# All attention scores from float32 words, with a head's two halves of keys on the two halves of the array's rows

## The chip, the cores and the metric

The kernel runs on one core of a Trainium2 chip. A core has TensorE (PE, matrix products out of on-chip memory SBUF into the accumulators PSUM), VectorE (DVE), ScalarE (ACT), GpSimd (POOL), a queue that issues transfers (SP), and 16 DMA engines that carry them. Each engine works through its own list of instructions in order and waits at semaphores for the others. The metric is the device time of one execution, in microseconds (us). The kernel before took 1036.89 us (median of 3 runs, 1036.31 to 1038.67).

## The reference

Attention of 4 batches x 8 heads, 576 queries and keys, 64 numbers to a head, with a threshold on the scores; then two layers, each a product into 2048 columns, a function, and a product back to 512 columns. All in float32.

```python
scores = scale * np.matmul(q, k.transpose(0, 1, 3, 2))           # 4 x 8 x 576 x 576, 64 terms to a sum
thresh = np.max(scores, axis=-1, keepdims=True) - tau
scores = np.where(scores >= thresh, scores, -1000000000.0)
attn = np.exp(scores - np.max(scores, axis=-1, keepdims=True))
attn = attn / (np.sum(attn, axis=-1, keepdims=True) + 1e-09)
x = np.matmul(attn, v)                                            # heads side by side: 2304 x 512
h = x @ w_in;   sp = log1p(exp(h));   x = (h * tanh(sp)) @ w_out  # first layer
h = x @ w_in2;  x = (h * clip(h + 3, 0, 6) / 6) @ w_out2          # second layer
```

A score that is slightly wrong can fall on the other side of the threshold, so the scores are computed to float32's precision. The other products use pairs of float16 numbers (a high and a low part, three products).

## The kernel before

**A planner sets the order.** Every piece of work is a task with the engines that may do it, a cost, the tasks it needs, the buffers it holds and a due time (lines 150 to 330). `Plan.run` takes the tasks in the order of a model of the engines and writes each engine's list accordingly. The constants at the top of the file (`STEP`, `START`, `EASE`, `WHO` and so on) are due times and weights of this planner; `BUFS`, `PV_DEEP` and `BANKS` are the numbers of buffers. A buffer's next user waits until its last reader is done. The trace has the lists as they then ran.

**Attention** goes batch by batch, in each through four pairs of heads. A pair has four blocks of 128 queries, two tiles each (one per head), and a block with the last 64 queries of both heads, one tile: 9 tiles a pair, 36 a batch, 144 in all. A tile passes: scores on PE (`scores`, L1479) into a buffer `s` of two banks, 288 keys in each; maximum on DVE (`peak`, L1488); threshold and exponential on ACT (L1493, L1498); mask and sum on DVE (`mask`, L1501), which frees `s`; a float16 high part on ACT (L1506) and a low part on POOL (`p_lo`, by the helper at L387); a transposing DMA (L1514) that turns the tile's keys into rows (`pt`); and the product with the values on PE (`pv`, L1527, 28 products for two heads). There are two buffers `s`, three each of `e` and `p16`, two of `pt`. Normalised blocks are flipped (L1643) into the input of the first layer.

**The scores were computed in two ways.** In batch 0 (`direct`), q and k are loaded as float32 on rows 0 to 63 of the array and multiplied as they are: one float32 product for each half of the keys. In batches 1 to 3, q and k are loaded twice, one copy on each half of the rows, and split into a high and a low part in a shorter format (`float32r`): `k_hi` and `q_hi` on ACT (L1391, L1384), `q_lo` on DVE or POOL (the helper L387), `k_lo` on DVE (L1394). With the parts stacked on 128 rows, two products for each half of the keys give the same precision: four a tile.

**The first layer** runs behind the attention. Products with `w_in` (`gemm1`, L865) are dealt out in small pieces between the attention's products, block by block of 256 tokens as they come out; their results go to DRAM (`hd`). Once the attention is over come the function (Mish) and the products with `w_out` (`gemm2`, L979), then the second layer (L1052, L1199). Weights arrive as 64-bit words and are converted on DVE, ACT and POOL (`convert`, `one_conversion`, L446 to L600). Those of `w_out` (`convert(1, ...)`) lie in memory that the attention's buffers of the pool `early` had held, so that their conversion can begin only when batches 0 to 2 are planned.

## Time and profile before

| | us |
|---|---|
| median of 3 runs | 1036.89 (1036.31 to 1038.67) |
| the profiled execution | 1039.59 |
| its span, first to last instruction | 1037.4 |
| PE busy | 959.5 (92%) |
| DVE busy | 776.5 (75%) |
| ACT busy | 672.2 (65%) |
| POOL busy | 548.5 (53%) |
| attention, start of its last scores in the trace | 428.8 |

Busy time counts an instruction from its start to its end. PE's products overlap in the pipeline, so how many it can do is read from the distance between their starts, not from the length of one. TensorE's clock is either at 2.4 GHz or at 1.2 GHz; the profile's column PEclk is the granted share of the higher one.

### The profile page before, as it was taken

Reading aid. Unit: us, or ns where it says so; the run is one execution under the profiler, and the core shown is the slowest. Engines: PE = TensorE matmul, PEld = TensorE weight load, DVE = VectorE, ACT = ScalarE, POOL = GpSimd, SP = SyncE. Lnnn points to the kernel's source line nnn. Section 1 sums busy time; section 2 is a strip of 40 time slices with the busy share of each in tenths; the row PEclk is TensorE's granted clock in tenths of the full one; section 3 lists DMA queues with packets and bytes.
Section 4 is the critical chain, followed back from the end, with each engine's and each line's share of the span. In section 5 each row is a group of like instructions: output and inputs, shape, how many; then the busy total and the mean of one; then the engine's idle time right before and its main releaser. Section 6 shows DMA issues by size and latency. Waiting matters only on the chain.

```text
span 1037.4 us, 25967 instructions
## 1 busy us (share of the span) xinstructions
PE 959.5 (92%) x10776; PEld 853.8 (82%) x10776; DVE 776.5 (75%) x1454; ACT 672.2 (65%) x1058; POOL 548.5 (53%) x421
## 2 busy tenths in 40 slices
PE   4879898999898998899999999989899999999996
PEld 2556577888788877798888888889899999999986
DVE  5887787887877879768888889889647747746754
ACT  5666587788788878666778787736436435536542
POOL 1667666566666567663667788742323324224332
PEclk9996689999999999899999999999999999999998
DMA  9685769999999999987656565753011101101001
GB/s 269 187 173 133 180 147 245 200 236 221 221 226 222 207 243 226 211 297 255 227 199 219 207 251 199 259 215 143 21 38 57 38 22 58 57 2 57 22 2 42
DMA packets 199333, 166.83 MB, mean 161 GB/s; under 512 B 174128, under 2 KB 174640, under 8 KB 192816
## 3 DMA queue, kind: packets, MB, share of 16 engines
q1 hardware_dynamic: 199216, 165.18, 60.2%
q8 instruction: 85, 1.39, 0.6%
q14 instruction: 32, 0.26, 0.1%
HBM read 86.64 MB, written 36.04 MB: 118 GB/s over the span
## 4 chain that ended last, share of the span: by engine, by line
PE 65%; DMA 12%; DVE 10%; ACT 4%; issue 4%; POOL 3%; SPq 0%; DVEq 0%; POOLq 0%; ACTq 0%
PE y_y L979 16%; DMA pt_tr<-p_ph 10%; PE h_g L865 10%; PE s_s L1479 7%; PE h_g0a L1052 4%; PE hp_g1a L1052 4%; PE aux_pv L1527 3%; POOL p_ph L387 2%; PE hp_g1d L1052 2%; PE h_g0d L1052 2%; DVE e_ex L1501 1%; PE h_g1b L1052 1%; ACT e_ex L1498 1%; PE y_y__1_8_0_15376 L1199 1%; PE y_y___1_1_0_11177 L1199 1%
## 5 line engine op out<-in xcount | busy, mean ns | idle before, releaser
L387 POOL TENSOR_TENSOR p_ph<-e_ex,p_ph 128x128 f16<-128x128 f32 (+3 forms) x160 | 187.1, 1191 | 103.2 <-ACT p_ph L1506 84.6
L387 POOL TENSOR_TENSOR gs_h<-g_ab,gs_h 128x896 f16<-128x896 f32 x36 | 94.5, 2639 | 219.4 <-ACT gs_h L1149 219.1
L1052 PEld LDWEIGHTS <-w__h 128*128 128x128 f16 x2016 | 157.5, 98 | 7.6 <-issue 6.9
L1199 PEld LDWEIGHTS <-gs_h 128*128 128x128 f16 x1512 | 146.4, 98 | 18.0 <-DVE out_va L1243 1.4
L1488 DVE TENSOR_REDUCE nm_pk<-s_s 128x1 f32<-128x576 f32 x144 | 105.2, 750 | 37.7 <-PE s_s L1479 37.0
L1501 DVE SCALAR_TENSOR_TENSOR e_ex<-s_s,thr_th,e_ex 128x576 f32<-128x576 f32 x144 | 111.9, 812 | 21.5 <-ACT thr_th L1493 16.5
L1498 ACT ACTIVATE e_ex<-s_s,nm_pk 128x576 f32<-128x576 f32 x144 | 104.3, 733 | 24.4 <-DVE nm_pk L1488 15.2
L1527 PE MATMUL aux_pv<-vh,pt_tr 128*128 128x65 f16 (+1 forms) x1296 | 89.9, 206 | 23.2 <-DMA pt_tr<-p_ph 21.8
L1527 PEld LDWEIGHTS <-pt_tr 128*128 128x128 f16 x2016 | 83.4, 104 | 33.7 <-DMA pt_tr<-p_ph 29.2
L1506 ACT ACTIVATE p_ph<-e_ex 128x576 f16<-128x576 f32 x144 | 94.9, 680 | 15.1 <-DVE e_ex L1501 7.0
L1052 PEld LDWEIGHTS <-w__u 128*128 128x128 f16 x1008 | 99.2, 98 | 1.0 <-issue 1.0
L1149 ACT ACTIVATE gs_h<-g_ab 128x1792 f16<-128x1792 f32 x36 | 59.9, 1690 | 38.0 <-DVE g_ab L387 38.0
L1133 ACT ACTIVATE g_ab<-g_ab,aux,hscales 128x512 f32<-128x512 f32 x72 | 54.1, 804 | 20.6 <-DVE g_ab L1080 20.6
L913 ACT ACTIVATE he_t<-h_g,hin 128x512 f32<-128x512 f32 x69 | 47.2, 685 | 23.3 <-PE h_g L865 19.4
L387 DVE TENSOR_TENSOR gs_h<-g_ab,gs_h 128x896 f16<-128x896 f32 x36 | 48.5, 1350 | 17.7 <-ACT gs_h L1149 17.7
L1080 DVE TENSOR_TENSOR g_ab<-h_g0d,s_ka 128x256 f32<-128x256 f32 x36 | 13.6, 419 | 58.9 <-PE h_g0d L1052 41.2
L959 DVE SCALAR_TENSOR_TENSOR gs_h<-hp_e,fscales,gs_h 128x512 f16<-128x512 f32 x72 | 51.4, 742 | 6.6 <-ACT gs_h L953 6.6
L1139 DVE SCALAR_TENSOR_TENSOR g_ab<-g_ab,f 128x512 f32<-128x512 f32 x72 | 52.5, 767 | 2.5 <-ACT g_ab L1133 2.5
L1479 PE MATMUL s_s<-kda_lk,qsa_qp 64*128 64x288 f32 x80 | 36.5, 618 | 19.0 <-DVE e_ex L1501 9.4
L950 ACT ACTIVATE hp_e<-hl_l 128x512 f32<-128x512 f32 x72 | 41.5, 593 | 15.8 <-DVE gs_h L959 15.6
L953 ACT ACTIVATE gs_h<-hp_e,fscales 128x512 f16<-128x512 f32 x72 | 46.2, 679 | 7.2 <-PE y_y L979 5.1
L446 DVE TENSOR_REDUCE top<-raw_lr 128x1 f32<-128x1024 f32 x32 | 38.9, 1215 | 10.1 <-DMA raw_lr<-in_moe_w_out 5.5
(691 smaller groups left out, 2927.2 us busy)
## 6 DMA issues: line engine op xcount, KB each, us to landing
hd<-he_t SPq DMA_DIRECT2D x36, 512.0 KB, 3.7
hl_l<-hd SPq DMA_DIRECT2D x18, 1024.0 KB, 5.3
raw_lr<-in_moe_w_in SPq DMA_DIRECT2D x16, 1024.0 KB, 5.5
raw_lr<-in_moe_w_out SPq DMA_DIRECT2D x16, 1024.0 KB, 6.7
yd<-yl_zhy SPq DMA_DIRECT2D x9, 896.0 KB, 3.8
rk_lk<-in_k SPq DMA_DIRECT2D x12, 576.0 KB, 5.4
rq_lq<-in_q SPq DMA_DIRECT2D x12, 576.0 KB, 5.9
v_lv<-in_v SPq DMA_DIRECT2D x16, 320.0 KB, 5.8
```

Of the source, the lines that this page charges most:

```text
L387: engine[e].tensor_tensor(dst, a, b, ALU.subtract)
L865: mm(hv[:, j, :], wj[:, wl, c * P : (c + 1) * P], x.tile[:, c, xl, :], start=j == 0 and n == 0, stop=j == 1 and n == 11, skip_group_check= ...
L979: mm(yv[:, h, :], wt[1][f // 2].tile[:, f % 2, wl, c * P : (c + 1) * P], gs[fp // COL].tile[:, fp % COL, gl, f % 2, :], start=fp == 0 and ...
L1052: mm(dst.tile[:, i * Q : (i + 1) * Q], wt[2][fp][wl].tile[:, right - 1, c * P : (c + 1) * P], x[xl].tile[:, c, left - 1], start=first and ...
L1149: nc.scalar.activation(part.tile[:, :, 0], g.tile[:, :, 1:], AF.Copy)
L1199: mm(region(p), part[:, gl, left - 1], wt[3][fp][wl].tile[:, right - 1], start=fp == n == 0 and spot(p)[1] == 0, stop=fp == NG - 1 and n == 2,
L1479: mm(s[j].tile[:, half, :HALF], lh, rh[:, half * HALF : (half + 1) * HALF], start=m == 0, stop=m == len(terms) - 1,)
L1488: nc.vector.tensor_reduce(neg.tile[:, j : j + 1], sv(j), AX.XY, ALU.max, negate=True)
L1498: nc.scalar.activation(ev(j), sv(j), AF.Exp, bias=neg.tile[:, j : j + 1])
L1501: nc.vector.scalar_tensor_tensor(ev(j), sv(j), thr.tile[:, j : j + 1], ev(j), ALU.is_ge, ALU.mult)
L1506: nc.scalar.activation(p16.tile[:, js, :S], e_.tile[:, js], AF.Copy)
L1527: mm(ov[:, dst, :d], pt.tile[:, j, ch, :], part.tile[:, src, vc, :], start=i == j == ch == 0 and part is vh, stop=j == w - 1 and ch == 8, ...
```

## The change

All 144 score tiles are now products of float32 words. k is laid out so that the first 288 keys of a head stand on rows 0 to 63 and the last 288 on rows 64 to 127; q stands on both halves. The two halves of the keys are then two products on the two halves of the array's rows, each into its own bank. The splitting into parts goes, with its buffers; k's load is half as large (288 KB a pair), q's stays at 576 KB, in batch 0 too (288 KB before). k is still multiplied by the scale on ACT, in half as many columns. The memory that this frees holds the converted `w_out` from the start, so that its conversion is no longer tied to the end of batch 2. The buffers `e` and `p16` go from 3 to 4, `pt` from 2 to 3. Batch 3 is planned like the others. The planner's constants have new values.

```diff
-PV_DEEP = 2
+PV_DEEP = 3
-BUFS = {"e": 3, "p16": 3}
+BUFS = {"e": 4, "p16": 4}
...
-    early = ExitStack()
-    ep = early.enter_context(tc.tile_pool(name="early", bufs=1, side="right"))
+    wpool_o = ctx.enter_context(tc.tile_pool(name="wpool_o", bufs=1))
...
-    r_rq = ring("rq", ap, 1, [P, 2, S])
-    r_rk = ring("rk", ap, 1, [P, 2, S])
-    r_qs = [ring("qs" + "ab"[k], (ap, ep)[k], 2, [P, 2, QW], F32R) for k in range(2)]
-    r_kd = [ring("kd" + "ab"[k], (ap, ep)[k], 2, [P, 2, S], F32R) for k in range(2)]
-    r_kld = [ring("kld" + "ab"[k], (ap, ep)[k], 2, [P, 2, S], F32R) for k in range(2)]
+    r_qs = ring("qs", ap, NPAIR, [P, 2, QW])
+    r_kd = ring("kd", ap, NPAIR, [P, 2, HALF])
...
+        def load_k(e):
+            nc.sync.dma_start(out=kd.tile, in_=k[n])
+        def load_q(e, js):
+            nc.sync.dma_start(out=qs.tile[:, js, :S], in_=q[n][:, js])
         def k_scaled(e):
-            nc.scalar.activation(words(kd), words(kd), AF.Copy, scale=qscale[:D])
+            nc.scalar.activation(kd.tile, kd.tile, AF.Copy, scale=qscale)
...
-            kh = prep({"act": 1.2}, k_hi, [lk], [rk, kd], "kh")
-            a = prep({"act": 1.155}, lambda e: q_hi(slice(0, 2)), [lq], [rq, qs], "qh")
-            for j in range(2):
-                ql.append(prep(both(S), lambda e, j=j: q_lo(e, j), [a], [rq, qs], f"ql{j}_"))
-            kl = prep({"dve": 1.42}, k_lo, [kh], [rk, kd, kld], "kl")
+        kl = prep({"act": 0.65}, k_scaled, [lk], [kd], "kh")
...
             def scores(j):
-                if direct:
-                    qt, ks = qs.tile[:D].bitcast(F32), [kd.tile[:D].bitcast(F32)]
-                else:
-                    qt, ks = qs.tile, [kd.tile, kld.tile]
                 if c < NQ:
                     q0 = j * TAIL + c * P
-                    terms = [(qt[:, j, q0 : q0 + P], k[:, j]) for k in ks]
+                    terms = [(qs.tile[:, j, q0 : q0 + P], kd.tile[:, j])]
...
-                for half in range(2):
-                    for m, (lh, rh) in enumerate(terms):
+                for m, (lh, rh) in enumerate(terms):
+                    for half, r in enumerate(side):
                         mm(
                             s[j].tile[:, half, :HALF],
-                            lh,
-                            rh[:, half * HALF : (half + 1) * HALF],
+                            lh[r],
+                            rh[r],
...
-    plan.run(before)
-    early.close()
-    wpool_o = ctx.enter_context(
-        tc.tile_pool(name="wpool_o", bufs=1, side="right", reuse_waits="tile")
-    )
-    convert(1, w1o, wpool_o, plan.clock["dve"] + OUT_AT, OUT_STEP * STEP, r_h)
+    convert(1, w1o, wpool_o, START + OUT_AT * STEP, OUT_STEP * STEP, r_h)
```

`side` is the pair of row ranges 0 to 63 and 64 to 127.

In PE's list, a place in batch 1 of the kernel before: a block's last products with the values, the scores of the block's two heads (`s_s_..._0_...` and `s_s_..._1_...`), and first-layer products.

```order
L1527 MATMUL aux_pv_4_0_1_1784<-vh_140,pt_tr_4_0_1_1668 128x130
L1479 MATMUL s_s_1_0_0_1803<-kda_kh_1_1255,qsa_qp_0_1095 128x288
L1479 MATMUL s_s_1_0_0_1803<-klda_kl_2_1508,qsa_qp_0_1095 128x288
L1479 MATMUL s_s_1_0_0_1803<-kda_kh_1_1255,qsa_qp_0_1095 128x288
L1479 MATMUL s_s_1_0_0_1803<-klda_kl_2_1508,qsa_qp_0_1095 128x288
L1479 MATMUL s_s_1_1_0_1814<-kda_kh_1_1255,qsa_qp_0_1095 128x288
L1479 MATMUL s_s_1_1_0_1814<-klda_kl_2_1508,qsa_qp_0_1095 128x288
L1479 MATMUL s_s_1_1_0_1814<-kda_kh_1_1255,qsa_qp_0_1095 128x288
L1479 MATMUL s_s_1_1_0_1814<-klda_kl_2_1508,qsa_qp_0_1095 128x288
L865 LDWEIGHTS w__h_6__1_1357
L865 MATMUL h_g_0_0_0_1_1687<-x_fl_0_2_438,w__h_6__1_1357 128x256
```

The same kind of place in the changed kernel's list, for the two heads of a block (`s_s_3_0_...` and `s_s_3_1_...`).

```order
L1486 MATMUL aux_pv_2_0_1_2805<-vh_136,pt_tr_2_1_1_2696 128x65
L1438 MATMUL s_s_3_0_0_2836<-kd_lk_0_1235,qs_qp_0_1230 128x288 x2
L860 LDWEIGHTS w__h_2__1_698
L860 MATMUL h_g_0_0_2_1_2801<-x_fl_0_2_1984,w__h_2__1_698 128x256
L860 LDWEIGHTS w__h_2__1_698
L860 MATMUL h_g_0_0_2_1_2801<-x_fl_0_2_1984,w__h_2__1_698 128x256
L1438 MATMUL s_s_3_1_0_2848<-kd_lk_0_1235,qs_qp_0_1230 128x288 x2
L860 LDWEIGHTS w__h_2__1_698
```

A tile's scores are two calls in place of four, and the two heads stand apart, with first-layer products between them. Counted over the whole list, the scores stood in 84 unbroken groups before, 20 of them in batch 0 and 64 in batches 1 to 3; now in 112, of 21, 29, 31 and 31 in the four batches, and 78 of them hold one tile. The calls number 80 a batch now; before 80 in batch 0 and 160 in each of the others.

In DVE's list, the first work of the kernel before: the maxima of the values (`vt_vm`) and of the first scores (`nm_pk`).

```order
L373 COPY istack<-ident 64x64
L1333 TENSOR_REDUCE vt_vm_0_1_194<-v_lv_0_0_168 128x1
L1488 TENSOR_REDUCE nm_pk_0_0_1_200<-s_s_0_0_0_182 128x1
L1333 TENSOR_REDUCE vt_vm_0_1_194<-v_lv_0_0_170 128x1
L1333 TENSOR_REDUCE vt_vm_0_1_194<-v_lv_0_0_172 128x1
L1333 TENSOR_REDUCE vt_vm_0_1_194<-v_lv_0_0_174 128x1
L1488 TENSOR_REDUCE nm_pk_0_0_1_200<-s_s_0_1_0_191 128x1
```

And that of the changed kernel.

```order
L371 COPY istack<-ident 64x64
L1447 TENSOR_REDUCE nm_pk_0_0_1_197<-s_s_0_0_0_186 128x1
L1447 TENSOR_REDUCE nm_pk_0_0_1_197<-s_s_0_1_0_192 128x1
L1460 SCALAR_TENSOR_TENSOR e_ex_0_0_2_205<-s_s_0_0_0_186,thr_th_0_0_1_208,e_ex_0_0_2_205 128x576
L1324 TENSOR_REDUCE vt_vm_0_1_212<-v_lv_0_0_177 128x1
```

The first scores' maxima and the first mask now stand ahead of the values' maxima.

In SP's list, transfers of the changed kernel at the end of batch 0 and in batch 1: the last load of `w_in` and the first of `w_out` (`raw_lr`), loads of k, q and v, transposes.

```order
L509 DMA raw_lr_7_0_1244<-in_moe_w_in 128x1024
L509 DMA raw_lr_0_0_1251<-in_moe_w_out 128x1024
L1342 DMA v_lv_2_0_1299<-in_v 128x640
L1631 DMA td<-xts_fl_4_2_1310 128x64
L1473 DMA_TRANSPOSE pt_tr_3_1_1_1351<-p_ph_3_0_1_1222 128x18x128
```

The first load of `w_out` now stands in the list as early as the end of batch 0, the next three up to the end of batch 1, the other four in batch 3; before, all eight stood in batch 3, the last two behind the attention's last transpose. On DVE the conversion of `w_out` has 16 long steps (two a group, the lines that were L567 and L572): 13 of them now stand ahead of the attention's last mask, 8 of these between the 50th and the 84th of its 144 masks; before, 6 of the 16, from the 125th mask on.

## Rows read from the trace of the kernel before

**Rows 1.** Stages: busy PE, PEld, DVE, ACT, POOL; clock, DMA share, GB/s.

```profile
0.00:145.00 145.00, 110.44 (x695) 77.09 (x696) 109.01 (x213) 92.04 (x150) 84.28 (x89) 0.85 0.72 181
145.00:437.00 292.00, 266.66 (x3266) 238.37 (x3267) 230.09 (x404) 237.01 (x430) 190.63 (x169) 0.98 1.06 222
437.00:690.00 253.00, 250.16 (x2365) 224.58 (x2363) 214.20 (x387) 182.86 (x269) 176.35 (x127) 1.00 0.67 235
690.00:750.00 60.00, 54.15 (x767) 51.35 (x764) 47.79 (x101) 31.25 (x43) 16.37 (x8) 0.97 0.26 94
750.00:1038.00 288.00, 278.10 (x3694) 262.44 (x3691) 175.40 (x353) 129.02 (x167) 80.87 (x30) 0.99 0.12 37
```

**Rows 2.** Who waited for whom, 145 to 437 us: total us, times, longest.

```profile
PEld L1527 <- DMA pt_tr<-p_ph: 25.9, 21, 2.7
PE aux_pv L1527 <- DMA pt_tr<-p_ph: 19.0, 19, 2.4
```

**Rows 3.** DMA, 145 to 437 us: packets, MB, share; issues, KB, landing us.

```profile
q1 hardware_dynamic: 137075, 64.22, 105.0%
...
raw_lr<-in_moe_w_out SPq DMA_DIRECT2D x5, 1024.0 KB, 7.1
...
pt_tr<-p_ph SPq DMA_TRANSPOSE x62, 5.5
```

**Rows 4.** Scores by form: count, shortest/median/longest ns, first and last start.

```profile
L1479 PE MATMUL s_s<-kda_lk,qsa_qp x80: 402/684/847, 6.9 to 104.3; 64*128 64x288 f32 x80
L1479 PE MATMUL s_s<-kdb_lk,qsb_qp x80: 402/684/846, 38.4 to 144.5; 64*128 64x288 f32 x80
L1479 PE MATMUL s_s<-kda_kh,qsa_qp x140: 288/297/589, 158.6 to 428.8; 128*128 128x288 f32 x140
```

**Rows 5.** PE by time, batch 0: start, length, line, tiles, shape, count.

```profile
102.19 0.38 PE L865 MATMUL h_g<-x_fl,w__h__1_420 128*128 128x256 f16 x2
102.50 2.20 PE L1479 MATMUL s_s<-kda_lk,qsa_qp 64*128 64x288 f32 x8
104.55 1.13 PE L1479 MATMUL s_s<-kdb_lk,qsb_qp 64*128 64x288 f32 x4
105.61 0.61 PE L865 MATMUL h_g<-x_fl,w__h__1_420 128*128 128x256 f16 x4
```

**Rows 6.** The same view, an earlier stretch of batch 0.

```profile
31.86 4.17 PE L1479 MATMUL s_s<-kda_lk,qsa_qp 64*128 64x288 f32 x8 [1.44 <-DVE e_ex L1501]
```

**Rows 7.** The same view, batch 1.

```profile
209.30 0.38 PE L1479 MATMUL s_s<-kda_kh,qsa_qp 128*128 128x288 f32 x1
209.51 0.29 PE L1479 MATMUL s_s<-klda_kl,qsa_qp 128*128 128x288 f32 x1
...
210.31 0.29 PE L1479 MATMUL s_s<-klda_kl,qsa_qp 128*128 128x288 f32 x1
210.44 0.61 PE L865 MATMUL h_g<-x_fl,w__h__1_1357 128*128 128x256 f16 x4
```

**Rows 8.** Chain that ended last, 0 to 145 us, shares by line.

```profile
by line: PE s_s L1479 30.4%; issue 8.0%; PE h_g L865 6.7%; DVE e_ex L1501 6.0%; DMA kdb_lk<-in_k 6.0%; PE aux_pv L1527 5.4%; DMA raw_lr<-in_moe_w_in 5.3%; POOL p_ph L387 3.9%; DMA pt_tr<-p_ph 3.3%; DVE nm_pk L1488 2.6%; SPq L1405 1.6%; POOL
```

**Rows 9.** Splitting of k and q, and batch 0's scaling of k, by form.

```profile
L1391 ACT ACTIVATE kda_kh<-rk_lk,qscale x8: 1240/1256/1260, 86.4 to 378.1; 128x1152 fp32r<-128x1152 f32 x8
L1384 ACT ACTIVATE qsa_qp<-rq_lq x7: 1150/1161/1181, 133.1 to 380.7; 128x1152 fp32r<-128x1152 f32 x7
L1394 DVE SCALAR_TENSOR_TENSOR klda_kl<-rk_lk,qscale,kda_kh x8: 1406/1408/1529, 112.9 to 379.4; 128x1152 fp32r<-128x1152 f32 x8
L1408 ACT ACTIVATE kda_lk<-kda_lk,qscale x2: 1254/1254/1254, 5.4 to 8.2; 64x1152 f32<-64x1152 f32 x2
```

**Rows 10.** The low part of q on POOL.

```profile
L387 POOL TENSOR_TENSOR qsa_qp<-rq_lq,qsa_qp x14: 1403/1413/2272, 140.1 to 387.5; 64x576 fp32r<-64x576 f32 x14
```

**Rows 11.** Conversion of weights on DVE, two of a group's three long steps.

```profile
L446 DVE TENSOR_REDUCE top<-raw_lr x32: 1202/1214/1226, 18.3 to 665.0; 128x1 f32<-128x1024 f32 x32
L567 DVE SCALAR_TENSOR_TENSOR cvt_c__1_329<-raw_lr,cvt_c__1_329 x1: 1215/1215/1215, 38.9 to 38.9; 128x1024 uint32<-128x1024 uint32 x1
```

154 lines of the change are left out of this document (60 added, 94 removed).

## Prediction

> **What bounds the kernel now.** I read the stages first [rows 1]. From 437 us on PE does little but work: 250.2 us busy of 253, and 278.1 of 288 after 750. What is left there is first- and second-layer products, whose number does not change. Only the attention, up to 437, and the short dip from 690 to 750 (54.2 of 60) can move. So I ask of each edit: how many microseconds sooner or later does PE get through the attention with the products dealt out in it?
>
> The two parts of the attention differ. Batch 0 takes 145 us, a later batch 292 / 3 = 97. In batch 0 the scores alone are 30.4% of the chain that ends last, 44 us [rows 8]. Their float32 records are 64 rows high, two to each product: the 160 records [rows 4] answer to 80 products. At the higher clock four of them take 1.13 us, the last with its 0.40 us to the end, so they start (1.13 - 0.40) / 3 = 0.243 us apart [rows 4, 5]; at 31.86 us eight take 4.17, or 0.52 each [rows 6], the lower level of the two (1.2 and 2.4 GHz), in a stretch where PE had just waited 1.44 us for DVE; over all of batch 0 the granted clock is put at 0.85 [rows 1]. A tile of four records is 0.97 us at the higher clock and about 2 at the lower.
>
> In batches 1 to 3 no engine is full and none is idle: PE 266.7 of 292, ACT 237.0, DVE 230.1, POOL 190.6 [rows 1]. The DMA share is 1.06, and the transposes land 5.5 us after their issue [rows 3]; PE's longest waits are for them, 19 times 19.0 us in all, seen also at its weight loads [rows 2]. So PE has about 25 us of slack there, made by transposes that come late.
>
> **Fewer float32 records in a row: batch 0.** The two halves of the keys now stand on different rows. If PE works on both halves at once, and takes its list in order, then a lone tile, whose records stand as half 0, half 0, half 1, half 1, can overlap only the second with the third: three slots of 0.243 us for four. In a longer group each neighbouring pair of unequal halves overlaps, so that m products take m + 1 slots, where they took 2m. No row shows two halves at once, so the bounds are the nearest rows: no overlap (2m slots, as now [rows 5]) and complete overlap (m). I take m + 1, since it needs only that neighbours on different rows overlap.
>
> The Trainium skill ("TensorE: Matmul & The Clock Gate", Part 3) says that matmuls on different row groups run at the same time and start in program order, some 4 ns apart; no run here shows it.
>
> In batch 0 the changed list has 80 products in 21 groups: 101 slots for 160. The chain's 44 us become 44 x 101 / 160 = 28, a gain of 16 us. No overlap gives 0, complete overlap 44 / 2 = 22. What is late next is DVE: 109.0 us of work [rows 1] in 145 - 16 = 129 us, a share of 84%, above the 79% of the later batches. The list lets DVE start on scores before it waits for the values, which helps it to that share. So I let the 16 stand; at 22 it would have to reach 89%.
>
> **More PE time in batches 1 to 3.** There a product of split parts is one record on 128 rows, 0.133 us apart; eight of them, entry included, take 210.44 - 209.30 = 1.14 us, so entry costs at most 1.14 - 8 x 0.133 = 0.08 [rows 7]. All of it: 480 x 0.133 + 64 groups x 0.08 = 69 us. The 64-row records have a dearer entry: the product before them starts at about 102.30 (the second of two, 0.11 apart), its 0.11 us end at 102.41, the next one after twelve records starts at 105.61; 3.20 - 12 x 0.243 leaves 0.28 us for entry and exit [rows 5]. The changed list has 240 products in 91 groups: (240 + 91) x 0.243 + 91 x 0.28 = 80 + 25 = 106 us. That is 37 us more for PE.
>
> The Trainium skill ("TensorEngine Tiling (Array Packing)", Key Properties) says that a change of tiling mode drains TensorE, which speaks against a list that goes to and fro 112 times. The trace agrees so far as the exit costs too: the last record starts at 104.55 + 3 x 0.243 = 105.28 and is over at 105.52, 0.09 us before the next product [rows 5]. By the rule the sum is as above; if only the first float32 weight load cost, the 0.19 us that are left, it would be 8 us less.
>
> Behind each score group wait first-layer pieces and products with the values on PE's list, and behind the latter the flips. What covers the 37 us is the slack of 25 us; I charge the rest, +12. Bounds: with complete overlap the cost is 240 x 0.243 + 25 - 69 = +15, which the slack covers: 0. With none it is 480 x 0.243 + 25 - 69 = +73, less 25: +48. If the slack covers nothing, +37. Deeper buffers (`e`, `p16`, `pt`) let more transposes be under way; since the DMA engines are at a share of 1.06 already, I give that nothing, but it is the reason why the slack may shrink without cost.
>
> **What goes from the other engines.** ACT loses 12 x (1.25 + 1.16) and 4 x 1.25 us and gets 16 scalings of half the columns, by the row of 1.25 us for 1152 about 0.63 each (an estimate): 34 - 10 = 24 us less. DVE loses 12 x 1.41 = 17, POOL 24 x 1.41 = 34 [rows 9, 10]. But half of it comes back: 7 of the 16 long steps of `w_out`'s conversion move into the attention, 3.5 groups with three steps of 1.2 us each on DVE [rows 11], 13 us, and as much again on ACT and POOL together. The loads: ten of k in the window lose 288 KB each, 2.9 MB of 64, and some three or four of `w_out` at 1 MB come in [rows 3]; so the DMA share stays. None of these engines sets the pace in batches 1 to 3 beside PE and the transposes, so 0; the bounds are -12 (the relief gives back what is charged above) and +4 (1 MB more where the share is over 1, at 222 GB/s 4.5 us).
>
> **The dip from 690 to 750.** It is where the second layer starts while DVE still converts and splits: DVE 47.8 of 60 busy, PE 5.9 idle [rows 1]. The 13 us of conversion that leave the stretch after 437 let that work end sooner: -4, bounds 0 and -6. The end, after 750, has new constants but the same work: 0, within 3 either way.
>
> **Sum.** -16 + 12 - 4 = -8. On the profiled execution, 1037.4 us of span and 2.2 around it, that is 1039.6 - 8 = 1031.6. The median of the runs lies 2.7 below that execution, and the forecast is given on the runs' scale: 1029 us.
>
> **Rivals.** Under 0.2% (2.1 us) this kernel's measurement can't tell a change from none.
>
> 1. *Overlap in order, slack used* (the forecast): 1029, by itself 1014 to 1044. Chance 0.47, of it 0.36 faster, 0.04 same, 0.07 slower.
> 2. *Complete overlap.* The halves run side by side even in a lone tile. Batch 0 gains up to 22, batches 1 to 3 lose nothing: 1036.9 - 22 - 4 = 1011. For it: the order of the four records may not matter if each half of the rows has its own queue. Against it: DVE's 109 us in batch 0. Chance 0.18, all faster.
> 3. *PE becomes the bound of batches 1 to 3* (slower). Place: the 91 score groups there. Price: the 37 us show in full, because the waits for late transposes [rows 2] fall at other times than the extra records; it decides from the point where slack hides less than 17 of them, since then more than the 20 us gained elsewhere show. -16 + 37 - 4 = +17: 1054. For it: PE is already the busiest engine, and lone tiles pay entry and exit each. Chance 0.17.
> 4. *No overlap*, the change does not do what it says: the halves run one after the other as two 64-row records each. Batch 0 gains nothing, batches 1 to 3 lose 48, the dip gives 4: +44, 1081. For it: nothing in the trace shows two records at once, and a float32 record may fill a resource that both halves need. Chance 0.13.
> 5. *The transposes set the pace throughout* [rows 2, 3], and batch 0's gain is lost in later waits: 1036. Chance 0.05, nearly all same.
>
> Together: faster 0.36 + 0.18 = 0.54; same 0.04 + 0.04 = 0.08; slower 0.07 + 0.17 + 0.13 + 0.01 = 0.38. The range takes in cases 1, 2 (at its likely end) and 3 with 12 us beyond it, and leaves out case 4 and the tails: 1008 to 1066.
>
> **What will show it.** Start distances of the 64-row records: a lone tile's four records at 0, 0.243, about 0.247, 0.49 for the forecast; 0, 0, 0.24, 0.24 for rival 2; 0, 0.24, 0.49, 0.73 for rival 4. The first layer's piece behind a lone tile should start about 1.0 us after the end of the piece before it. Batch 0's last mask should come some 16 us earlier, and the scores' share of the chain before it fall to about 28 us. Busy PE time in batches 1 to 3 should rise to over 95% of them if rival 3 holds. The dip should keep under 3 us of idle. I am wrong if records on different rows start no closer than records on the same rows, if DVE holds batch 0 near 145 us, or if batches 1 to 3 lengthen by more than 25 us.

## The result, and the profile after

The changed kernel takes 1011.38 us (median of 4 runs, 1009.38 to 1013.25) where the kernel before, beside it, takes 1036.60: a ratio of 0.9756, 95% interval 0.9725 to 0.9788. The forecast was 1029: the direction was right, the size was not, 25 us where 8 were predicted. The profiled execution took 1009.65 us, 1007.9 of it the span; before, the span was 1037.4. Three runs that stand far from the others of their kernel (4219 us in e16 below, and 1391 and 1613 us of the kernel before, measured beside e13 to e16) are left out of the ratios.

The stages of the profile after, which answer to [rows 1] (columns as there):

```profile
0.00:145.00 145.00, 93.31 (x850) 62.89 (x850) 122.97 (x235) 100.56 (x172) 90.62 (x97) 0.80 0.89 229
145.00:437.00 292.00, 282.47 (x3351) 218.72 (x3347) 226.53 (x421) 225.85 (x418) 173.64 (x156) 1.00 0.97 213
437.00:690.00 253.00, 248.98 (x2493) 224.90 (x2491) 214.06 (x394) 181.72 (x268) 155.11 (x110) 1.00 0.65 231
690.00:750.00 60.00, 59.75 (x783) 56.21 (x782) 35.12 (x72) 25.95 (x32) 17.92 (x7) 1.00 0.08 26
750.00:1008.00 258.00, 248.90 (x3312) 234.84 (x3309) 162.59 (x328) 118.48 (x154) 75.39 (x28) 0.99 0.11 36
```

From 145 to 437 us PE is busy 282.5 us of 292 where it was 266.7. What PE itself waits for there longest (total us, times, longest):

```profile
PE s_s L1438 <- DVE e_ex L1460: 3.5, 4, 1.3
PE s_s L1438 <- DVE top L455: 1.7, 2, 1.2
```

No wait of PE or its weight loads for a transpose is listed in that stretch any more: the 19.0 and 25.9 us of [rows 2] are gone.

To place the gain I mark the end of each batch by the end of its 36th mask (`e_ex`) on DVE, and count the first-layer products that PE has started by the last mask, since PE fills its gaps with them. The last masks of the attention, before and after:

```profile
431.09 0.81 DVE L1501 SCALAR_TENSOR_TENSOR e_ex<-s_s,thr_th,e_ex 128x576 f32<-128x576 f32 x1
```

```profile
415.05 0.81 DVE L1460 SCALAR_TENSOR_TENSOR e_ex<-s_s,thr_th,e_ex 128x576 f32<-128x576 f32 x1
```

| us | before | after | difference |
|---|---|---|---|
| batch 0 ends | 148.7 | 129.1 | -19.6 |
| batches 1 to 3 last | 283.2 | 286.8 | +3.6 |
| first-layer products done by then | 1205 | 1276 | +71 |
| from there to the second layer's first product | 252.0 | 243.7 | -8.3 |
| from there to the end of the span | 353.5 | 348.3 | -5.2 |

The four times add to -29.5, the difference of the two profiled spans; the medians differ by 25. The -8.3 is no gain of that stage: a first-layer product takes PE 0.113 us in batch 1 (53.3 us for 470), and 71 of them, 8.0 us, were done earlier. The 71 are a difference too: batch 0 does 66 where it did 93, and batches 1 to 3 do 1210 where they did 1112. With every product counted where it was done before, batch 0 gains 16.5 us, batches 1 to 3 gain 7.5, the stretch to the second layer 0.3.

The overlap is plain in PE by time (start, length, line, tiles, shape, count). A lone tile of the changed kernel, which answers to [rows 5]:

```profile
201.83 0.49 PE L860 MATMUL h_g<-x_fl,w__h__1_545 128*128 128x256 f16 x3
202.25 0.76 PE L1438 MATMUL s_s<-kd_lk,qs_qp 64*128 64x288 f32 x4
202.94 0.44 PE L1606 MATMUL aux_fl<-istack,xtail 128*128 128x64 f32 x2
```

Four records are through in 0.76 us where four on the same rows took 1.13. Singly they start at 202.255, 202.261, 202.601 and 202.609: two at once, and again two at once. All 70 lone tiles of batches 1 to 3 do so; the medians of their four starts are 0, 0.007, 0.347 and 0.354 us. The product behind such a tile starts 0.78 us after the end of the piece before it, where the prediction looked for 1.0. The kernel asks for half 0 and then for half 1, two records each. The trace does not name a record's rows, so that a pair is one record of each half is concluded from e1 below, where all are on the same rows and none starts less than 0.24 us behind another. Whether the halves ran out of the list's order, or stood interleaved in the list as PE got it, no view shows.

How long PE is busy with the scores, in batch 0 and after it, before and after the change (stretch, its length, busy PE with its records, clock, DMA share, GB/s; these instructions alone):

```profile
0.00:148.70 148.70, 72.50 (x164) 0.85 0.71 177
148.70:437.00 288.30, 81.93 (x476) 0.98 1.07 224
```

```profile
0.00:129.10 129.10, 42.02 (x164) 0.78 0.89 229
129.10:437.00 307.90, 82.21 (x476) 1.00 0.97 214
```

Batch 0's scores shrink by 30.5 us. In the later batches busy time stays as it was, but there it misleads: it counts each record to its end, past the start of the product behind it, and leaves out the way in. What a group of scores costs PE is the time from the end of the product before it (its start and the usual distance to the next of its kind, 0.109 us for the first layer's) to the start of the product behind it. Summed over the groups of batches 1 to 3 from the starts in the traces, with PE's idle time taken off (the stretches are those of the last table):

| batches 1 to 3, us | before | after | difference |
|---|---|---|---|
| groups of scores in the trace | 64 | 90 | +26 |
| the scores, start to start | 71.3 | 85.3 | +14.0 |
| PE idle | 25.3 | 9.7 | -15.6 |
| first-layer products | 1112 | 1210 | +98 |
| length | 283.2 | 286.8 | +3.6 |

So the scores did grow, by 14.0 us, where the prediction charged 37 and gave 15 as its bound for complete overlap. (e18 below, with the same list of scores, gives 88.2, so the sum is good to some 3 us.)

The start differs too. DVE by time, before and then after: before, the maxima of the values stand ahead in its list and wait 6.12 us for their transfer, while the first scores are done.

```profile
10.33 0.82 DVE L1333 TENSOR_REDUCE vt_vm<-v_lv 128x1 f32<-128x640 f32 x1 [6.12 <-DMA v_lv<-in_v]
11.07 0.75 DVE L1488 TENSOR_REDUCE nm_pk<-s_s 128x1 f32<-128x576 f32 x1
11.73 2.26 DVE L1333 TENSOR_REDUCE vt_vm<-v_lv 128x1 f32<-128x640 f32 x3
13.91 0.75 DVE L1488 TENSOR_REDUCE nm_pk<-s_s 128x1 f32<-128x576 f32 x1
...
15.96 1.54 DVE L1501 SCALAR_TENSOR_TENSOR e_ex<-s_s,thr_th,e_ex 128x576 f32<-128x576 f32 x2 [1.05 <-ACT thr_th L1493]
```

```profile
7.24 0.76 DVE L1447 TENSOR_REDUCE nm_pk<-s_s 128x1 f32<-128x576 f32 x1 [2.49 <-PE s_s L1438]
8.20 0.76 DVE L1447 TENSOR_REDUCE nm_pk<-s_s 128x1 f32<-128x576 f32 x1 [0.20 <-PE s_s L1438]
9.32 0.82 DVE L1460 SCALAR_TENSOR_TENSOR e_ex<-s_s,thr_th,e_ex 128x576 f32<-128x576 f32 x1 [0.36 <-ACT thr_th L1452]
10.13 1.64 DVE L1324 TENSOR_REDUCE vt_vm<-v_lv 128x1 f32<-128x640 f32 x2
```

The first mask ends at 10.1 us in place of 16.8, and batch 0 has 6.7 us more.

### The profile page after: what moved, and what is told of

It is laid out like the page before. It is cut to its first block, busy times and chain, and to the rows that moved or that the text cites. A ratio compares the mean times of both kernels' runs of the same rounds, so it can differ in the third digit from the quotient of the medians.

```text
span 1007.9 us, 25906 instructions
## 1 busy us (share of the span) xinstructions
PE 933.4 (93%) x10776; PEld 797.6 (79%) x10776; DVE 761.3 (76%) x1448; ACT 652.6 (65%) x1040; POOL 512.7 (51%) x397
## 4 chain that ended last, share of the span: by engine, by line
PE 49%; DVE 3%; DMA 1%; ACT 0%; issue 0%; SPq 0%; DVEq 0%
PE y_y L974 16%; PE h_g0a L1047 4%; PE hp_g1a L1047 4%; PE hp_g1d L1047 2%; PE h_g0d L1047 2%; PE h_g L860 2%; PE hp_g0b L1047 1%; PE h_g1b L1047 1%; PE y_y__1_8_0_15049 L1194 1%; PE y_y___1_6_0_13953 L1194 1%; PE y_y___1_5_0_13296 L1194 1%; PE y_y___1_3_0_12088 L1194 1%; PE y_y___1_2_0_11537 L1194 1%; PE y_y___1_0_0_10327 L1194 1%; PE y_y___1_1_0_10850 L1194 1%; PE y_y___1_7_0_14561 L1194 1%
## 5 line engine op out<-in xcount | busy, mean ns | idle before, releaser
L385 POOL TENSOR_TENSOR p_ph<-e_ex,p_ph 128x128 f16<-128x128 f32 (+3 forms) x160 | 191.3, 1219 | 109.2 <-issue 61.7
L1438 PE MATMUL s_s<-kd_lk,qs_qp 64*128 64x288 f32 x640 | 124.2, 491 | 35.1 <-DVE e_ex L1460 17.7
L1438 PEld LDWEIGHTS s_s<-kd_lk,qs_qp 64*128 64x128 f32 x640 | 59.0, 208 | 67.9 <-issue 32.5
L1465 ACT ACTIVATE p_ph<-e_ex 128x576 f16<-128x576 f32 x144 | 95.2, 680 | 18.5 <-DVE e_ex L1460 17.1
L1486 PE MATMUL aux_pv<-vh,pt_tr 128*128 128x65 f16 (+1 forms) x1296 | 87.3, 204 | 7.2 <-DMA pt_tr<-p_ph 7.0
L1486 PE MATMUL aux_pv<-vl_vl,pt_tr 128*128 128x64 f16 x720 | 71.1, 204 | 0.0
L908 ACT ACTIVATE he_t<-h_g,hin 128x512 f32<-128x512 f32 x69 | 46.8, 684 | 25.4 <-PE h_g L860 21.6
L385 DVE TENSOR_TENSOR gs_h<-g_ab,gs_h 128x896 f16<-128x896 f32 x36 | 46.9, 1304 | 19.5 <-ACT gs_h L1144 19.5
```

The lines of the kernel that those rows point to most:

```text
L385: engine[e].tensor_tensor(dst, a, b, ALU.subtract)
L1438: mm(s[j].tile[:, half, :HALF], lh[r], rh[r], start=m == 0, stop=m == len(terms) - 1,)
L1465: nc.scalar.activation(p16.tile[:, js, :S], e_.tile[:, js], AF.Copy)
L1486: mm(ov[:, dst, :d], pt.tile[:, j, ch, :], part.tile[:, src, vc, :], start=i == j == ch == 0 and part is vh, stop=j == w - 1 and ch == 8, ...
```

## The experiments

Two kinds must be kept apart. In some kernels the order of the instructions kept is exactly that of the kernel they come from (e1, e4, e13, e14, e15, e17, e18). The others were planned anew, and a new plan moves the time by itself. "Ratio" is to the kernel before in the same session.

| run | ratio, 95% | batch 0 ends | last mask | products by then | second layer starts | span |
|---|---|---|---|---|---|---|
| before | | 148.7 | 431.9 | 1205 | 683.9 | 1037.4 |
| after | 0.976 [0.973, 0.979] | 129.1 | 415.9 | 1276 | 659.6 | 1007.9 |
| e1 | 1.060 [1.056, 1.065] | 150.6 | 501.3 | 1276 | 745.0 | 1093.7 |
| e2 | 1.001 [0.999, 1.003] | 131.0 | 427.7 | 1344 | 678.3 | 1040.6 |
| e3 | 0.979 [0.976, 0.982] | 119.6 | 409.0 | 1278 | 661.1 | 1014.2 |
| e4 | 0.990 [0.987, 0.993] | 137.7 | 419.5 | 1205 | 670.0 | 1024.7 |
| e5 | 1.001 [0.999, 1.003] | 149.9 | 426.9 | 1207 | 684.2 | 1038.3 |
| e6 | 0.988 [0.985, 0.992] | 121.5 | 420.1 | 1260 | 675.5 | 1027.9 |
| e7 | 1.024 [1.020, 1.027] | 136.7 | 455.2 | 1300 | 708.3 | 1062.9 |
| e8 | 1.015 [1.011, 1.019] | 130.5 | 443.1 | 1344 | 696.9 | 1057.1 |
| e9 | 0.990 [0.987, 0.993] | 132.7 | 426.1 | 1276 | 681.0 | 1029.5 |
| e10 | 0.990 [0.987, 0.994] | 129.9 | 416.1 | 1289 | 677.9 | 1027.7 |
| e11 | 1.014 [1.010, 1.017] | 134.7 | 439.9 | 1344 | 691.0 | 1051.7 |
| e12 | 0.981 [0.976, 0.985] | 118.6 | 408.7 | 1294 | 662.2 | 1015.1 |
| e13 | 1.002 [1.000, 1.004] | 151.5 | 435.0 | 1204 | 685.6 | 1039.2 |
| e14 | 0.986 [0.983, 0.989] | 129.6 | 427.4 | 1276 | 671.1 | 1020.0 |
| e15 | 0.981 [0.978, 0.984] | 132.1 | 426.9 | 1276 | 670.6 | 1019.0 |
| e16 | 0.972 [0.969, 0.974] | 126.0 | 413.1 | 1276 | 656.8 | 1006.4 |
| e17 | 0.982 [0.978, 0.985] | 134.2 | 426.1 | 1276 | 669.8 | 1016.2 |
| e18 | 0.997 [0.995, 0.999] | 134.9 | 441.1 | 1276 | 684.8 | 1033.5 |

**The overlap, in an unchanged order.** The edits are shown in part; `...` marks a gap, and what stands behind `#` in them is a note. First the changed kernel with both halves on the same rows.

```diff
-                            lh[r],
-                            rh[r],
+                            lh[side[0]],
+                            rh[side[0]],
```

> The changed kernel with one edit: both halves of a tile's scores are multiplied on rows 0 to 63 (so the second half repeats the scores of the first half's keys; loads, scaling, buffers and the order of all instructions stay). Nothing can run side by side on two row groups any more. Theory 1 (the gain comes from complete overlap of the two row halves): a tile of four records takes 4 x 0.243 + 0.28 = 1.25 us of TensorE where the changed kernel's trace shows 2 x 0.243 + 0.28 = 0.77; a pair of heads (eight tiles and one with twice the records) 10 x 0.486 = 4.9 us more, twelve pairs of batches 1 to 3 58 us, four pairs of batch 0 19 us at the upper clock and up to 39 at the lower. TensorE is busy 255 of the 265 us from 145 to 410, so of the 58 about 50 come through, and batch 0 gets its 20 back: about 1,080 us (1,060 to 1,095). Rival A (the gain comes from ACT, DVE and POOL, which no longer split k and q, or from the deeper buffers): nothing of that is touched, so within 10 us of the changed kernel's 1,011.

1101.0 us, 6 beyond theory 1's range; rival A fell. The batches grow by 21.5, 22.5, 18.5 and 22.8 us. A lone tile of four records, by time:

```profile
210.65 1.23 PE L1438 MATMUL s_s<-kd_lk,qs_qp 64*128 64x288 f32 x4
211.81 0.39 PE L860 MATMUL h_g<-x_fl,w__h__1_960 128*128 128x256 f16 x2
```

From its first record to the next product it is 1.16 us where the two halves side by side take 0.69. In batches 1 to 3 the scores take 144.8 us of PE, start to start, where they take 85.3. So without the overlap the changed kernel is slower than the kernel before, for all its relief of the other engines.

Then the overlap put into the kernel before, in batch 0 alone (e4) and in batches 1 to 3 alone (e13). The edit of e13, where `pieces` has the terms outside and the halves inside; e4 does the same where `direct` holds, and loads each half of k to its own rows and q to all rows.

```diff
-                for half in range(2):
-                    for m, (lh, rh) in enumerate(terms):
...
-                            lh,
-                            rh[:, half * HALF : (half + 1) * HALF],
+                for half, (m, (lh, rh)) in pieces:
+                        r = slice(0, D) if direct else side[half]
...
+                            lh[r],
+                            rh[r, half * HALF : (half + 1) * HALF],
```

> The kernel before with one part of the change: in batch 0, where scores already come from float32 words, the halves of the keys go to rows 0 to 63 and 64 to 127; batches 1 to 3 keep their split words, buffers and numbers. Theory 1: the records of the two halves overlap fully, a tile takes two slots where it took four, and batch 0 loses 16 to 22 us, all of which reaches the end: 1,015 to 1,022 us, the last mask of batch 0 at 127 to 133 where it was at 148.7. Rival A (relief of the other engines or buffers made the gain): batch 0 is bound by ACT or DVE, 1,031 to 1,037 us.

1027.3 us, between the two cases: batch 0 ends 11.0 us earlier, not 16 to 22, and 12.4 reach the last mask. The scores' busy time falls as expected, from 72.50 to 39.34 us:

```profile
0.00:137.70 137.70, 39.34 (x164) 0.80 0.82 200
```

But of these 33 us only 11 show. PE's idle time in batch 0 rises from 34.6 to 58.3 us, the granted clock over it falls from 0.85 to 0.80, and the start is 2.3 us later (first mask at 19.1): DVE waits 7.77 us for the values in place of 6.12. Beside them q's load is twice as large here and k's comes in two transfers for each pair; which of these delays them is not shown. The changed kernel's batch 0 is 8.6 us better than this; its first mask comes 9.0 us earlier, and it holds 32 fewer first-layer products (66 for 98), 3.6 us of PE's work.

> The kernel before with batches 1 to 3's scores alone changed: one float32 product for each half of the keys on its half of the rows, in place of two products of split parts on all rows (it multiplies the rounded high words, so the scores are not the reference's); splitting, loads, buffers, numbers and the order of all other instructions stay. It measures by itself the step that the prediction put at +12 us (37 us more of TensorE, 25 of them covered). Theory 1 (complete overlap): the scores of these batches take 75 to 78 us of TensorE's time where they took 70.5, the last mask comes within 4 us of 431.9, and the time is 1,032 to 1,042. As the prediction had it (overlap in order): about 100 us, last mask some 12 later, 1,045 to 1,055.

1040.57 us, ratio 1.0016 [0.9996, 1.0035]; batches 1 to 3 last 283.5 us where they lasted 283.2. How long PE is busy with the scores there:

```profile
151.50:440.00 288.50, 77.95 (x476) 0.99 1.06 226
```

That is 4.0 us less than before; dealt out as each record's advance of PE's end, as the expectation counts it, it is 74.0 for 70.5. Start to start, which is the prediction's own measure, the scores take 80.3 us for 71.3: 9.0 more, not 37. The time does not show them. PE is idle 19.5 us of these batches where it was 25.3, for it waits less for transposes (19.0 us before):

```profile
PE aux_pv L1530 <- DMA pt_tr<-p_ph: 13.1, 15, 1.9
```

And the granted clock from 145 to 437 us is 0.99 where it was 0.98. So in this order the step that the prediction put at +12 us is 0, and the slack covers it, as the prediction's bound for complete overlap had it. The order is the old one, with 64 groups of scores; what the changed kernel's 91 groups cost beside them is not tested.

**The relief of ACT, DVE and POOL.** First with the splitting's work put back and planned anew: a copy of q on ACT, two halves on DVE or POOL, one whole subtraction on DVE.

```diff
...
+            h = prep({"act": 1.155}, again, lq[:1], [qs, sc], "dh")
+            lows = [prep(both, lambda e, j=j: less(e, j), [h], [qs, sc, sd], f"dl{j}_") ...]
+            kl = prep({"dve": 1.42}, more, lows + [kl], [qs, sc, sd], "dk")   # e7
+            prep({"dve": 1.42}, more, lows, [qs, sc, sd], "dk")               # e11
```

> The changed kernel with the splitting's work put back beside it for the twelve pairs of batches 1 to 3: a copy of q on ACT, two half subtractions on POOL or DVE and one whole subtraction on DVE, into tiles nobody reads, with the scores waiting for them as they waited for k's low part before. Theory 1 (these engines did not set the pace): within 6 us of the changed kernel, 1,005 to 1,018. Rival A (relief of ACT, DVE and POOL is why batches 1 to 3 did not lengthen): the last mask of batch 3 comes 12 to 25 us later than at 415.9, and the time is 1,023 to 1,037.

> As the run with the splitting's work put back, but no score waits for it. It took 39 us in the attention; either the three engines have no room for 12 x 1.16 us on ACT, 12 x 1.4 on DVE and 24 halves on DVE or POOL, or the scores wait for a chain of one buffer. Theory 3 (room on the engines): still over 1,035 us, last mask of batch 3 after 432. Rival F (the wait alone): within 10 us of 1,011.

1064.4 and 1053.8 us: theory 1 fell, e7 lies far beyond rival A's range too (1,023 to 1,037), and the wait explains only some 11 us of it. But both were planned anew, and 16 and 20 us of the loss lie behind the last mask. So the same loads were put into the changed kernel without the planner's knowledge, behind instructions that are there anyway, which leaves its order as it is.

```diff
             nc.scalar.activation(kd.tile, kd.tile, AF.Copy, scale=qscale)
+            if b > 0:
+                nc.scalar.activation(idle_act, idle_act, AF.Copy)              # e14, e18
+                nc.scalar.activation(idle_act[:, 0], idle_act[:, 0], AF.Copy)
...
+                nc.vector.scalar_tensor_tensor(                                 # e15, e18
+                    idle_dve, idle_dve, qscale, idle_dve, ALU.mult, ALU.subtract)
...
+                nc.gpsimd.tensor_tensor(part, part, part, ALU.subtract)         # e17, e18, twice
```

> The changed kernel with 1.9 us more of ACT work (copies of a tile nobody reads) behind each of the 12 scalings of k in batches 1 to 3, 23 us in all, about what ACT was relieved of; the order of all other instructions is exactly the changed kernel's, so no new plan is mixed in. If ACT's relief pays: the last mask 8 to 20 us later, 1,019 to 1,031. If ACT has room: within 4 us, 1,009 to 1,016.

> The same for DVE: 1.41 us more behind each of the 12 low parts of the values in batches 1 to 3, 17 us in all, what DVE was relieved of; order unchanged. If DVE's relief pays: the last mask 8 to 17 us later, 1,019 to 1,029. If DVE has room: within 4 us, 1,009 to 1,016.

> The changed kernel, order unchanged, with two subtractions of 64 x 576 (1.41 us each by the trace of before) on POOL behind each of the 12 pads of q in batches 1 to 3: 34 us, what POOL was relieved of. ACT's 23 us cost 12.0 in the same test, DVE's 17 us 7.0. If POOL's relief pays as theirs (half of it): 1,022 to 1,032. If POOL has room (160 us busy of 265): within 5 us, 1,008 to 1,016.

> All three at once, order unchanged: 22 us on ACT, 18 on DVE, 34 on POOL (in smaller tiles). If the prices add: 12 + 7 + POOL's, 1,030 to 1,045, so the relief of the three engines would be worth as much as the whole gain of the change or more. If they overlap, since one stall covers another: near the dearest alone, 1,023 to 1,029.

1023.4, 1018.4, 1019.5 and 1035.1 us. The added instructions of the first three (count: shortest/median/longest ns, first and last start):

```profile
L1382 ACT ACTIVATE idle_act<-idle_act x12: 1146/1151/1164, 75.9 to 358.2; 128x1152 f32<-128x1152 f32 x12
L1383 ACT ACTIVATE idle_act<-idle_act x12: 682/683/686, 77.1 to 359.4; 128x576 f32<-128x576 f32 x12
```

```profile
L1405 DVE SCALAR_TENSOR_TENSOR idle_dve<-idle_dve,qscale x12: 1409/1414/2304, 113.1 to 359.7; 128x1152 f32<-128x1152 f32 x12
```

```profile
L1386 POOL TENSOR_TENSOR idle_pool<-idle_pool x24: 1137/1144/2017, 72.0 to 327.9; 64x576 f32<-64x576 f32 x24
```

22 us on ACT lengthen batches 1 to 3 from 286.8 to 297.8, 17 on DVE to 294.8, 27 on POOL to 291.9, all three to 306.2: 11.0, 8.0, 5.1 and 19.4 us, so four fifths of the single prices' sum of 24.1. ACT paid as its first case had it, DVE too, with a time 0.6 us under that range; POOL lies between its two cases. The rest of each difference is in batch 0, which ends 0.5, 3.0, 5.1 and 5.8 us later: the first of the added loads run there, from 72 us on, as the first of the splitting did before, and the extra tiles are cleared there. In e18 PE is idle 23.3 us of batches 1 to 3 in place of 9.7. Its wait for the masks grows from the 3.5 us above, from 145 to 437 us:

```profile
PE s_s L1456 <- DVE e_ex L1478: 9.8, 10, 2.5
PE h_g L860 <- ACT he_t L908: 5.3, 3, 2.8
```

No engine is full in e18 (from 145 to 440 us: PE 273 us of 295, DVE 239, ACT 233, POOL 192), and yet each microsecond added on ACT or DVE alone costs about half of one. e18 as a whole is 0.3% below the kernel before: in the changed kernel's order, the loads put back at these places take nearly all of the gain. In another order a part is there without any relief: e4 won 1% that way.

**The buffers and the planner's numbers.** All planned anew.

In e3 and e6 the conversion of `w_out` does not keep its instant, as the expectation of e3 has it: `START + OUT_AT * STEP` goes from 293 to 272 in the planner's time. In e12 it is kept.

```diff
-PV_DEEP = 3                  # e2, e6: 2
-BUFS = {"e": 4, "p16": 4}    # e2, e6: 3, 3 (e5: the reverse, in the kernel before)
-STEP = 2.822                 # e3, e6, e12: 2.554, and START, EASE, ALPHA, WINDOW, ... of before
-V_FIRST = -1.379             # e16: -0.631
-CONV_STEP = 1.284            # e16: 0.905
-CONV_AT = 1.74               # e16: 2.3
```

> The changed kernel with before's depths: two in place of three transposed tiles of probabilities, three in place of four buffers of exponentials and of their 16-bit copies. Theory 1 (overlap alone): the waits for transposes return in part (21.8 us in 145 to 437 before, 7.0 now) but stand beside other work: 1,009 to 1,018 us. Rival B (the deeper buffers took the waits of 21.8 and 25.9 us for transposes out of batches 1 to 3, and that is why these batches did not grow): 1,025 to 1,045 us, and the last mask of batch 3 over 12 us later than at 415.9.

> The kernel before with the deeper buffers alone: three in place of two transposed tiles of probabilities, four in place of three buffers of exponentials and 16-bit copies; scores, splitting and all numbers as before. Theory 1 (overlap in every batch, and an earlier start, made the gain; depth matters only through the order that the planner finds): 1,028 to 1,042 us, the last mask of batch 3 at 428 to 434 where it was at 431.9. Rival B (depth itself took the waits for transposes away): the waits of 21.8 us in 145 to 437 fall under 12, the last mask comes by 420, and the time is 1,012 to 1,025.

> The changed kernel with before's buffer depths and before's planner numbers together: only the new scores, the loads without splitting and the early place of the output weights' conversion are left. Theory 1: the loss of 28 us with old depths and new numbers was a misfit of the two (a bad order where the second layer starts, not a lack of buffers), so with both old it is near the run with old numbers alone, 1,016: 1,010 to 1,024, last mask by 413. Rival B (depth): it is slow again, 1,030 to 1,045, last mask over 420.

> The changed kernel's program with the planner's numbers of before (step, start, costs of lateness, who may do what, windows), so that the same work is put in the order that the old numbers give; the instant of the output weights' conversion stays as it is in the changed kernel. Theory 1 (overlap alone): the numbers are worth little, 1,008 to 1,022 us; the later start (9.7 for 3 in the planner's own time) may cost up to 7 of it at the front. Rival C (the new numbers are what moved the first layer's work into the attention stage and shortened batches 1 to 3): 1,025 us or more.

The old depth costs some 27 us with the new numbers (e2, 1040.0; ratio 1.001 for 0.976) and some 10 with the old (e6 1027.2, e3 1016.3); the new depth gives the kernel before nothing (e5, ratio 1.0007). Theory 1 was right on the times of e3 and e5 (in e5 the last mask came 1.1 us before its range). It was wrong on e2, and by 3 us on e6, whose last mask came where rival B had it, 420.1. Rival B's time held for e2 alone, and not for its reason: PE's waits for transposes from 145 to 437 us are 1.0 us in e2. (The 21.8 and 7.0 us in the expectations of e2 and e5 are not of that stretch: there it was 19.0 before, and none is listed after.) Of the 32.7 us by which the span of e2 is longer than the changed kernel's, 11.8 come before the last mask, 6.9 from there to the second layer and 14.0 behind its first product. PE's longest waits stand where the second layer begins (655 to 690 us):

```profile
PE h_g0a L1047 <- DMA xl_x__1_0_0_9772<-yd: 7.1, 1, 7.1
PE h_zps L417 <- ACT dgb_zds L412: 6.4, 1, 6.4
```

In the changed kernel the longest such waits from 640 to 690 us are 1.6 and 1.0:

```profile
PE h_zpy L417 <- ACT dgb_zdy L412: 1.6, 1, 1.6
PE h_g0a L1047 <- DMA xl_x__1_0_0_9714<-yd: 1.0, 1, 1.0
```

In e2 68 more first-layer products (7.7 us) were spent before the last mask, and behind it PE is idle 13.4 us until the second layer, 0.3 in the changed kernel. That these products are what PE then lacked is likely and not shown. Depth and numbers are tied to each other through the order; what depth is worth by itself stays open.

> The changed kernel with the numbers of before for the attention and those of the changed kernel for what follows. With all numbers of before the attention ended at 409.0 where it ends at 415.9 in the changed kernel, with as many first-layer products done, but 13 us more went by from there to the end (PE idle 9.2 us before the second layer's first product, and a lower clock after it). If the two sets can be told apart so, the last mask stays by 411 and the rest takes 592 to 597: 1,002 to 1,010 us, faster than both. If what follows depends on the whole order, not on its own numbers, the rest takes 600 or more: 1,011 to 1,020.

> The changed kernel with three numbers of before, in its own steps (when the first values are loaded, and when and how fast the first weights are converted). With all numbers of before batch 0 ended at 119.6, with 18 fewer first-layer products, where it ends at 129.1. If these three made that and the rest of the plan keeps its shape: last mask by 410, 1,003 to 1,009 us, faster than both. If the plan moves as a whole, as it did in the runs with a new plan so far, the stretch after the attention grows by 5 to 13 us: 1,011 to 1,022.

e12: 1018.7 us. The attention ended at 408.7, as hoped, but 606 us came behind it: the stretch depends on the whole order. e16: 1009.3 us, just past its first case, as is its last mask, 413.1. It is faster than the kernel before; its ratio of 0.972 [0.969, 0.974] overlaps the changed kernel's, so it can't be told from it. Batch 0 ended at 126.0, not at 119.6: these three numbers explain a part at most.

**The values' maxima, and the output weights' place.** Both planned anew.

```diff
+                behind = first_tops[: 1 + 3 * j] if n == 0 and c == 0 else []
-                a = go({"dve": 0.75}, lambda e, j=j: peak(j), [a], ...)
+                a = go({"dve": 0.75}, lambda e, j=j: peak(j), [a, *behind], ...)           # e9
-            a = loaded = load_words(task, raw, src[g], f"lr{m}_{g}")
+            a = loaded = load_words(task, raw, src[g], f"lr{m}_{g}", barrier)  # e8, e10: barrier = batch 2's end
-OUT_AT = 102.714
+OUT_AT = 125                                                                              # e10
```

> The changed kernel with the maxima of batch 0's values put ahead of the first two scores' maxima on DVE, as the kernel before has them; there DVE waited 6.1 us for the values' transfer while the first scores were done, and its first mask ended at 16.8 us where the changed kernel's ends at 10.1. Theory 2 (part of batch 0's gain is this earlier start, beside the overlap: the run with halves in batch 0 alone won 11 of 19.6 us there and starts 9 us later): the first mask ends 5 to 8 us later, batch 0's last mask comes at 134 to 137 where it was at 129.1, and the time is 1,016 to 1,020. Rival (the start is caught up within batch 0): last mask of batch 0 within 2 us of 129.1, time 1,009 to 1,014.

> The changed kernel with the loads of the first layer's output weights, and so their conversion, held back until batch 2's attention is done, about where they stood before. Theory (the conversion that was moved forward shortened the stretch where the second layer starts): attention ends as before or up to 4 us earlier (less work in batches 1 and 2), the stretch from the second layer's first product to the end grows from 348.3 back to about 353, and the time is 1,012 to 1,018. Rival D (its place is free either way): within 2 us of 1,011. Rival E (a conversion in batch 3 delays the first layer's second products, which need these weights, and PE runs dry): over 1,020.

> As the run with the output weights held back until batch 2's attention is done, but with due times moved back too, so that the planner spreads their conversion over batch 3 and the first layer's rest, as the kernel before does, where that run did all of it in a rush within batch 3 (130 us long for 94.5). Theory 3 (the early place pays because DVE, ACT and POOL have room in batches 1 and 2 and none in batch 3): batch 3 takes 98 to 110 us, and the time is 1,018 to 1,035. Rival D (the rush alone was at fault): 1,009 to 1,016.

e9: 1030.4 us, outside both ranges. Batch 0 ends only 3.6 us later, so the 6 us are half caught up there; but batch 2 takes 105.7 us with 60 more first-layer products, and PE stands idle 9.5 us between the last mask and the second layer. A start 6 us later gave another plan, and that cost more than the start. The worth of the earlier start is not settled by it.

e8: 1054.2 us, over rival E's bound; the rush makes batch 3 130 us long. e10: 1029.8, in theory 3's range, but not for its reason. Batch 1 takes 90.5 us in place of 100.5 with 82 fewer first-layer products (9.3 us of work), batch 3 104.4 in place of 94.5 with 74 more (8.4 us): the attention is done at 416.1 as in the changed kernel, and the conversion's place costs it 2 us at most. The loss comes behind it, 17.6 us of idle PE before the second layer, the longest

```profile
PE h_zps L417 <- ACT dgb_zds L412: 7.5, 1, 7.5
```

So holding the conversion back cost 15 to 18 us in e10's plan and more in e8's; in e10 at the seam to the second layer and not in the attention. Behind the second layer's first product it is 349.8 us, 1.5 more than in the changed kernel, where I had expected 353.

## Why the prediction was wrong

**Batch 0, -16: right in sign and size, by another sum.** It ends 19.6 us earlier with 27 fewer first-layer products, which makes 16.5, so that the sizes agree is in part luck. The products take m slots, not m + 1, but of the 33 us that PE saves only 11 arrive (e4). For the other 8.6 there are three candidates and no run that parts them: the first mask comes earlier (in e9's new plan 6.1 us at the first mask were 3.6 at the end of the batch), fewer products are done, and the splitting for batch 1, which began in batch 0, is gone (put back in e18, batch 0 ends 5.8 us later). That DVE would be next, at 84%, is borne out by its share, 109.55 us of 129.1; that it sets the pace there is not shown, but in e15 two added steps and a clearing, 4.7 us on DVE, cost batch 0 3.0.

**"More PE time in batches 1 to 3", +12: the step that failed.** The overlap was wrong in it: in lone tiles only the second and third record were to overlap, which makes 106 us against 69, 37 more. The runs show complete overlap (starts at 0, 0.007, 0.347 and 0.354 us, not 0, 0.243, 0.247 and 0.49), 14.0 us more in the changed kernel and 9.0 in the old order, and 0 for this step by itself in the old order (e13). The prices were right, and so was the bound that they gave for complete overlap, +15 and covered by the slack; I gave that case too small a chance. The Trainium skill ("TensorE: Matmul & The Clock Gate", Part 3) was right that products on different row groups run at the same time. Whether they also start in program order can't be told here, since no view shows the rows of a record; I took it to mean that a tile's two halves overlap by one record only, and that was wrong. The rule of the drain ("TensorEngine Tiling (Array Packing)", Key Properties) is not contradicted: of the 0.78 us of a lone tile 0.29 are left for entry and exit beside two distances of 0.243, as the prediction had it.

**"What goes from the other engines", 0: mis-sized as well.** I argued that no engine but PE and the transposes set the pace, since none is full. Put back in the unchanged order, the three loads cost 19.4 us in batches 1 to 3 (e18). Together the two steps were to make +12; measured is -7.5 (3.6 us longer, with 98 more first-layer products inside, 11 us of work). That lies within the lower bound of -12, but far from the two tests, 0 (e13) and -19 (e18). PE's own account of these batches says where the rest went: its idle time fell by 15.6 us, the scores took 14.0 more, and the remainder, -5.9, is about what the granted clock makes (1.00 for 0.98 from 145 to 437 us, 2% of 283 us, an estimate). With 9.7 us of PE's idle time left, relief had little more to win; that is concluded from these sums and not tested by a run. The conversion's place explains 2 us at most (e10).

**The slack.** I said that it would cover 25 of 37 us. In e13 it does cover: PE's waits for transposes shrink from 19.0 to 13.1 us while the scores take 9.0 more. In the changed kernel they are gone. Deeper buffers alone did not remove them, 15.6 us of PE's 19.0 remain in e5; with the old depth they are 1.0 us (e2) and 7.8 (e6), and with the three loads put back none is listed either (e18). So neither the depth nor the relief is by itself the reason; the new order may be.

**The dip, -4: right in size**, -5.2 behind the second layer's first product; the reason is not shown. The second layer starts 24 us earlier now, so the same place is 665.7 to 725.7 us:

```profile
665.70:725.70 60.00, 58.90 (x863) 56.25 (x863) 45.81 (x100) 32.47 (x41) 18.03 (x7) 1.00 0.33 116
```

PE is idle 1.1 us there in place of 5.9, and the granted clock is 1.00 for 0.97. But DVE, which the conversion was to relieve, is nearly as busy as before, 45.8 us for 47.8, and with the conversion held back again (e10) only 1.5 of the 5.2 us return.

The sum by stages: predicted -16 + 12 - 4 = -8; measured, with every product in its old stage, -16.5 - 7.5 - 0.3 - 5.2 = -29.5. So two terms came out and the +12 did not. None of the prediction's three signs of being wrong came: records on different rows do start closer, batch 0 does not stay near 145 us, batches 1 to 3 lengthen by 3.6. The time came out where rival 2, complete overlap, had it (1011), to which I gave 0.18. Its mechanism was right; its sum, 22 us from batch 0 and nothing from the later ones, agrees only in total, and that is luck. The profile after gives no chain for the attention, so the scores' share of it is not known.

What stays open: how the gain of batch 0 divides beyond the 11 us of e4, what the lone tiles cost, what took away the waits for transposes, and what buffer depth is worth without a new plan.

## What to carry to other kernels

Products that overlap are priced by the distance between their starts: by busy time the later scores took the same (82.2 and 81.9 us), and that hid 14 us of PE. An engine that is not full can still cost time: with ACT and DVE at 77 and 78% of the stage, loads added to either came back at about half their size, so price relief by a test, and not by the engine's share. How much relief can still win, look for in the idle time of the busiest engine, here 9.7 us of 287. Where a planner sets the order, test an edit first in an order that does not change (work hidden from the planner, or the same list with other operands); a new plan can cost more than the edit, as in e9: 3.6 us at the end of batch 0, 21.6 at the end. And what an attention stage wins can be lost where the next stage runs dry, so look at that seam in each run.

## What was not expected of the hardware

Float32 products of 64 rows on the two halves of the array's rows ran in pairs that started 6 to 8 ns apart: a lone tile's four records take 0.69 us to the next product, on the same rows 1.16. In e13, at the same places as before, a further tile in a group adds 0.49 us, where the four split records of 128 rows that it replaces added 0.53. What costs more is the way in and out: a group of one tile took 0.22 us more than before, one of eight records 0.20, one of twelve 0.15. So full float32 words were nearly as quick here as the two split parts they replaced, and the more so the longer the group.
